# One more chunk's sums on TensorE and GpSimd, and preference for ten chunks' split steps, in a convolution with routed experts

## Chip, core and metric

The kernel runs on one core of a Trainium2 chip. The metric is the device time of one execution in microseconds (us). A profile of one execution goes with it: what every engine did and waited for.

## What is computed

Two stages. The first is a convolution over 7 past rows whose weights differ per token and head (a softmax over the 7 taps); the second sends each token to the one of 8 experts with the largest logit, and weights that expert's result with its softmax share.

```
B, S, D = 8, 3584, 192          # 28672 tokens; H = 8 heads of 24, K = 7 taps
w = softmax(weight_gen)                                        # (B, S, H, K)
x1[b, s, h] = sum_k w[b, s, h, k] * x_pad[b, s + k, h]         # 24 wide
logits = x1 @ w_gate                                           # 8 experts
e = argmax(logits);  gate = softmax(logits)[e]
out = gate * (relu(x1 @ w1[e]) @ w2[e])                        # 192 -> 1024 -> 192
```

## The kernel before, in words

**Tiling.** The tokens are cut into 28 chunks of 1024 (128 partitions with 8 tokens each), counted from 0 here: the fourth chunk is chunk 3. A chunk goes through three kinds of steps.

*Sums* (`taps`, `tap_ops`). The softmax weights `wp`, then for each of the 7 taps a product `x_sb * wp`. For a chunk from `HELP` on, VectorE (DVE) makes all 8 tokens' products (7 of 128x1536, lines 354) and adds them up itself (6 adds, line 378). For a chunk below `HELP`, VectorE makes only the products of 6 tokens (7 of 128x1152), TensorE (PE) adds them up by multiplying each with an identity into three PSUM tiles `ph` (line 363, 42 matmuls), and GpSimd (POOL) makes products and adds of the last two tokens (`wg`, `tp`, `acc`: 14 operations).

*Split* (`split`: `high`, then `low`). ScalarE (ACT) casts the sums to 16 bits into the row `pl` (line 448, or 444 from PSUM); VectorE writes what is left over (lines 461 and 463); TensorE transposes the 24 blocks (line 473), ScalarE copies them to `xg` (line 475).

*Finish* (`finish`). TensorE makes the logits in `pm` (line 485), VectorE routes (lines 492 to 507), counts and places, GpSimd sends the chunk's rows to the queues of the 8 experts in HBM (`send`, line 559, 8 indirect DMAs), and VectorE selects which tiles of tokens are now full (`choose`, the row numbers `rows`, line 599).

**Experts.** A tile has 256 tokens up to chunk 4 and 384 after it. SyncE (SP) loads its transposed rows `xt`, the expert's weights `wt` (1.8 MB, three buffers) and `meta`; TensorE makes the hidden layer (line 805) and the second layer (line 711), ScalarE takes results out of PSUM. A full tile needs 2040 waiting tokens while tiles have 256, more than 3064 with 384, so that chunk 1 gives one tile, chunks 2, 3 and 4 give four each, chunk 5 none and chunk 6 three.

**Weights.** All experts' weights are first split into two 16-bit parts by ScalarE (lines 271 and 272) and VectorE (lines 278 and 280), and written to `wq` in HBM (lines 285 to 290). This stretch, in which the first chunks are made too, is called the prologue here. A load of `wt` waits for all of `wq`.

**What sets the order.** A planner (`vector_step`) with a clock for VectorE and one for TensorE decides in which order the steps are written. In the prologue the framework then orders every engine by priorities and a simulated timeline; afterwards VectorE keeps the written order (`manual_schedule`) and the other engines are still ordered by the framework. `tc.high_priority()` puts the instructions written under it ahead of others that could go at the same time, on every engine that the framework orders. Only the finish steps ("route") are written under it. Each engine then works through its order and stops at an instruction whose input is not there.

The places that the change touches:

```
HELP = 3                                             # line 34
n = (J - POOL_COLS if c < HELP else J) * H           # line 342: tokens in wp
if c >= HELP:                                        # line 387: all on VectorE
```

Of the kernel before, what the change touches and what calls it, by code (L numbers as in the profile page):

```python
# [30 lines left out]
NCAP = 1 << 15  # L31
J = 8
POOL_COLS = 2
HELP = 3
EARLY = 5
STEP = 0.2
HURRY = 0.3
# [19 lines left out]
EXP_AT = 4  # L57
SC_AT = 7
MX_FROM = 3
SQ = 4  # L60
PROB = 3
TV = 2
# [51 lines left out]
def conv_moe_kernel(ctx: ExitStack, tc: tile.TileContext, x, wgen, w_gate, w1, w2, out):  # L114
# [203 lines left out]
    def soft0(c):  # L318
        k = ch[c]
        mx = cw.tile([P, J * H], F32, name="mx")  # L320
        nc.vector.tensor_reduce(mx, k.w, axis=AX.X, op=ALU.max)  # L321
        nc.gpsimd.tensor_tensor(k.w, k.w, mx.unsqueeze(2).to_broadcast([P, J * H, KW]), op=ALU.subtract)  # L322

    def soft1(c):
        nc.scalar.activation(ch[c].w, ch[c].w, AF.Exp)
# [12 lines left out]
    def soft3(c):  # L338

        k = ch[c]  # L340
        k.wp = ps_w.tile([P, J * H, KW], F32, name="wp")
        n = (J - POOL_COLS if c < HELP else J) * H
        nc.vector.tensor_tensor(k.wp[:, 0:n], k.w[:, 0:n], k.rs[:, 0:n].unsqueeze(2).to_broadcast([P, n, KW]),
                                op=ALU.mult)

    def tap_ops(eng, k, a, b, nm, aps):

        ac = k.acc[:, a:b, :].rearrange("p a (h g) -> p (a h) g", h=H)

        def mult(n, out):  # L350
            xs = k.x[:, a + n:b + n, :].rearrange("p a (h g) -> p (a h) g", h=H)
            w = k.wg if eng is nc.gpsimd else k.wp[:, a * H:b * H]
            ws = w[:, :, n:n + 1].to_broadcast([P, (b - a) * H, G])
            eng.tensor_tensor(out, xs, ws, op=ALU.mult)  # L354

        if aps is not None:
            for n in range(KW):
                t = cw.tile([P, (b - a) * H, G], F32, name=nm, bufs=TV)
                mult(n, t)
                tf = t.rearrange("p a g -> p (a g)")  # L360
                for i, ap in enumerate(aps):
                    m = min(2, b - a - 2 * i) * D
                    nc.tensor.matmul(ap[:, 0:m], identf, tf[:, 2 * i * D:2 * i * D + m],  # L363
                                     start=(n == 0), stop=(n == KW - 1))
                    clock[1] += 4 * m / 2400.0
                yield
            return
        mult(0, ac)
        yield
        t = cw.tile([P, (b - a) * H, G], F32, name=nm, bufs=TV)  # L370
        mult(1, t)
        yield
        for n in range(2, KW + 1):
            if n < KW:
                t2 = cw.tile([P, (b - a) * H, G], F32, name=nm, bufs=TV)
                mult(n, t2)
                yield
            eng.tensor_tensor(ac, ac, t, op=ALU.add)  # L378
            if n < KW:
                t = t2  # L380
            yield

    def taps(c):
# [4 lines left out]
        k.aps = None  # L388
        if c >= HELP:
            for _ in tap_ops(nc.vector, k, 0, J, "tv", None):  # L390
# [15 lines left out]
    def square(c, n, m):  # L406

        k = ch[c]

        def one(half, i, col, m):  # L410
            junk = cw.tile([P, m * D], BF16, name="junk", bufs=1, padded_shape=[P, J * D])
            v = k.x[:, col:col + m, :].rearrange("p a d -> p (a d)")
            nc.scalar.activation(junk, v, AF.Square, accum_out=ssqs[:, half, i:i + 1])  # L413

        if c == 0 and n == 0:
            one(1, 0, 0, HALO)
        one(c % 2, n // 2, HALO + n, m)
# [242 lines left out]
    def sums():  # L660
# [9 lines left out]
        for c in range(NCH):  # L670
# [4 lines left out]
            for cost in taps(c):  # L675
                n += 1
                if n <= 2 and c + 1 < NCH:
                    for i in range(4 * n - 4, 4 * n, SQ):
                        square(c + 1, i, SQ)
                yield cost, None  # L680
                if c + 1 < NCH:
                    if n == 2 and c + 1 < MX_FROM + 2:
                        soft0(c + 1)
                        yield 0.6, None
                    if n == EXP_AT:
                        soft1(c + 1)
                    if n == MX_AT and MX_FROM <= c < NCH - 2:

# [203 lines left out]

    def advance(queue_, what, after):
        at, g, c = queue_[0]
        with tc.high_priority() if what == "route" else nullcontext():
            lat = next(g, None)
        if lat is None:
            done[what] = c
            queue_.pop(0)
            if after:  # L900
                after(c)
        else:
            lat, cost = lat if isinstance(lat, tuple) else (lat, OP)
            clock[0] += cost
            queue_[0][0] = clock[0] + lat

    def vector_step():
# [12 lines left out]
        if routes and routes[0][0] <= now + (HURRY if routes[0][2] < SOON else 0.0):  # L920
            clock[0] = max(now, routes[0][0])
            advance(routes, "route", None)
            return True
        if splits and splits[0][0] <= now and splits[0][2] - done["route"] <= SPLITS:
            advance(splits, "split", lambda c: routes.append([clock[0], finish(c), c]))
            return True
# [77 lines left out]
```

## Time and profile before

| | us |
|---|---|
| median of 3 runs | 1240.84 |
| lowest to highest | 1239.42 to 1244.1 |
| profiled execution, its own time | 1242.18 |
| span of that execution in the trace | 1240.5 |
| PE busy | 1133.4 |
| DVE busy | 1036.7 |
| ACT busy | 696.8 |
| POOL busy | 660.6 |

The rows that the prediction uses come from that one execution. Times in them are counted from the start of the span; the 1.7 us between the span and the execution's own time lie outside it. A busy PE has a matmul under way, which is not the same as PE at its peak.

### The profile page before, as it was taken

To read this page: it belongs to the slowest core of one execution; us is meant where nothing else is said; L and a number is where in the kernel's file an instruction comes from. 1 tells how busy PE (TensorE), PEld (TensorE's weight loads), DVE (VectorE), ACT (ScalarE), POOL (GpSimd) and SP (SyncE) were. 2 spreads that over 40 slices of the span, in tenths; PEclk is the share of its full clock that TensorE was granted. 3 is DMA by queue.
4 is the path that set the end of the run, shared out by engine and by line. 5 is a ranking of instruction groups with operands and counts; after the bars stand their busy time and mean duration, and the time that the engine had idled before them with its cause. 6 is when DMAs were issued, how large, how long until landed. Compare 5 with 4: busy or idle time off the path is not lost.

```text
span 1240.5 us, 30087 instructions
## 1 busy us (share of the span) xinstructions
PE 1133.4 (91%) x11621; PEld 927.2 (75%) x11621; DVE 1036.7 (84%) x1849; ACT 696.8 (56%) x1459; POOL 660.6 (53%) x562
## 2 busy tenths in 40 slices
PE   5692189997999999999999999999999998999997
PEld 3461179896678788778788787787777786789997
DVE  7999966999999999999999999999998976232331
ACT  3455167675566666656756666656655663543442
POOL 6850853666656565446755565656464656222222
PEclk9896599999999999999999999999999999999998
DMA  9996698897768878787798878878776667999995
GB/s 277 346 323 241 232 282 264 287 304 236 232 201 267 265 230 250 238 234 235 247 277 237 237 227 255 247 240 254 239 215 178 191 197 222 340 348 348 321 362 218
DMA packets 185133, 320.93 MB, mean 259 GB/s; under 512 B 132752, under 2 KB 156434, under 8 KB 169118
## 3 DMA queue, kind: packets, MB, share of 16 engines
q1 hardware_dynamic: 162862, 273.68, 70.8%
q0 software_dynamic: 22128, 45.33, 11.1%
q8 instruction: 91, 1.49, 0.5%
q14 instruction: 52, 0.43, 0.1%
HBM read 236.17 MB, written 60.76 MB: 239 GB/s over the span
## 4 chain that ended last, share of the span: by engine, by line
PE 63%; DVE 13%; DMA 10%; issue 7%; POOL 4%; SPq 1%; ACT 1%; POOLq 0%; DVEq 0%; ACTq 0%
PE ph L805 29%; PE y L711 27%; DVE tv L354 4%; DVE acc L378 3%; DMA wt<-wq 3%; PE ph L473 2%; PE ph L818 2%; DMA f<-in_moe_w_dram 2%; POOL out_dram L559 2%; DMA xt<-queue 2%; DMA queue<-pl,pos 2%; DVE hl L828 1%; POOL queue L559 1%; PE ph L363 1%; PE pm L485 1%
## 5 line engine op out<-in xcount | busy, mean ns | idle before, releaser
L805 PE MATMUL ph<-xt,wt 128*128 128x384 f16 (+6 forms) x3880 | 578.8, 292 | 24.5 <-DMA wt<-wq 16.8
L711 PE MATMUL y<-wt,hh 128*128 128x192 f16 (+2 forms) x3696 | 504.5, 247 | 2.1 <-ACT o L715 2.1
L559 POOL DMA_INDIRECT out_dram<-o,meta x231 | 288.5, 1249 | 394.6 <-ACT o L715 349.0
L711 PE MATMUL y<-wt,hl 128*128 128x192 f16 (+2 forms) x1848 | 450.3, 247 | 0.4 <-ACT hl L820 0.2
L805 PEld LDWEIGHTS <-wt 128*128 128x128 f16 x3880 | 329.3, 98 | 144.4 <-DMA wt<-wq 18.9
L711 PEld LDWEIGHTS <-hh 128*128 128x128 f16 (+2 forms) x3696 | 337.0, 99 | 35.9 <-issue 5.0
L559 POOL DMA_INDIRECT queue<-pl,pos x224 | 286.8, 1280 | 118.1 <-issue 56.7
L828 DVE SCALAR_TENSOR_TENSOR hl<-ph,hh 128x384 f16<-128x384 f32 (+2 forms) x372 | 204.2, 562 | 144.2 <-ACT hh L825 139.0
L354 DVE TENSOR_TENSOR tv<-x_sb,wp 128x1536 f32<-128x1536 f32 (+1 forms) x171 | 289.0, 1693 | 3.9 <-PE ph L363 3.7
L825 ACT ACTIVATE hh<-ph 128x384 f16<-128x384 f32 (+2 forms) x372 | 185.5, 501 | 181.0 <-PE ph L805 170.4
L378 DVE TENSOR_TENSOR acc<-acc,tv 128x1536 f32<-128x1536 f32 x150 | 261.8, 1745 | 0.0
L711 PEld LDWEIGHTS <-hl 128*128 128x128 f16 (+2 forms) x1848 | 181.7, 98 | 16.5 <-ACT hl L820 1.4
L814 ACT ACTIVATE hh<-ph 128x384 f16<-128x384 f32 (+1 forms) x204 | 105.2, 518 | 84.7 <-PE ph L805 82.0
L715 ACT ACTIVATE o<-y,fac 128x192 f32<-128x192 f32 (+2 forms) x231 | 91.7, 418 | 89.4 <-PE y L711 83.4
L820 ACT ACTIVATE hl<-ph 128x384 f16<-128x384 f32 (+1 forms) x204 | 104.1, 519 | 37.0 <-PE ph L818 36.4
L475 ACT ACTIVATE xg<-ph 128x1024 f16<-128x1024 f16 x84 | 83.9, 1027 | 24.3 <-PE ph L473 24.2
L473 PE MATMUL ph<-idh,pl 128*128 128x128 f16 x672 | 56.1, 225 | 25.4 <-ACT pl L448 15.8
L818 PE MATMUL ph<-hh,negi 128*128 128x384 f16 (+1 forms) x256 | 68.1, 304 | 1.7 <-ACT hh L814 1.6
L473 PEld LDWEIGHTS <-pl 128*128 128x128 f16 x672 | 44.5, 101 | 29.4 <-ACT pl L448 16.1
L363 PE MATMUL ph<-tv,identf 128*128 128x384 f32 x126 | 51.6, 553 | 7.6 <-DVE tv L354 7.3
L413 ACT ACTIVATE junk<-x_sb 128x768 bf16<-128x768 f32 (+2 forms) x56 | 48.0, 857 | 13.6 <-DMA x_sb<-in_x_dram 6.5
L322 POOL TENSOR_TENSOR w_sb<-w_sb,mx 128x448 f32<-128x448 f32 x28 | 29.7, 1062 | 45.5 <-DVE mx L321 43.6
(121 smaller groups left out, 780.7 us busy)
## 6 DMA issues: line engine op xcount, KB each, us to landing
wt<-wq SPq DMA_DIRECT2D x97, 1796.0 KB
x_sb<-in_x_dram SPq DMA_DIRECT2D x27, 1344.0 KB
w_sb<-in_weight_gen_dram SPq DMA_DIRECT2D x28, 224.0 KB
wq<-ws SPq DMA_DIRECT2D x8, 772.0 KB
f<-in_moe_w_dram SPq DMA_DIRECT2D x8, 768.0 KB
f<-in_moe_w_dram SPq DMA_DIRECT2D x8, 512.0 KB
wq<-ws SPq DMA_DIRECT2D x8, 512.0 KB
wq<-ws SPq DMA_DIRECT2D x32, 128.0 KB
```

The lines of the kernel that those rows point to most:

```text
L354: eng.tensor_tensor(out, xs, ws, op=ALU.mult)
L378: eng.tensor_tensor(ac, ac, t, op=ALU.add)
L473: nc.tensor.transpose(pt[:, m, :], p16[:, j, n * P:(n + 1) * P], idh)
L559: st = nc.gpsimd.indirect_dma_start(out=dst, out_offset=bass.IndirectOffsetOnAxis(ap=idx, axis=0), in_=src, in_offset=None, **kw)
L711: nc.tensor.matmul(y, hx[:, f, sl], w2v[:, f, t, :], start=(f == 0 and k == 0), stop=(f == NF - 1 and k == 2))
L715: nc.scalar.activation(o[0:m, :], y, AF.Copy, scale=fac[0:m, s:s + 1])
L805: nc.tensor.matmul(ph[:, g], wt[:, wc + f * P:wc + (f + 1) * P], xt[:, xc, 0:T], start=(k == 0 and g == 0), stop=(k == 4), skip_group_chec ...
L814: nc.scalar.activation(hv, ph, AF.Relu, scale=SHRINK)
L818: nc.tensor.matmul(ph[:, g], negi, hv[:, g], start=False, stop=True, skip_group_check=True)
L820: nc.scalar.activation(lv, ph, AF.Relu)
L825: nc.scalar.activation(hv, ph, AF.Relu)
L828: nc.vector.scalar_tensor_tensor(lv, ph, 0.0, hv, op0=ALU.max, op1=ALU.subtract)
```

## The change

`HELP` goes from 3 to 4, so that chunk 3 too is summed by TensorE, with its last two tokens on GpSimd. A new constant `FRONT` of 10 puts the split steps of chunks 0 to 9 (and the steps of finishing, as before) under the priority. What is written under `advance` with `what` "split" are `high` and `low`.

```diff
-HELP = 3
+HELP = 4
...
+FRONT = 10
...
     def advance(queue_, what, after):
         at, g, c = queue_[0]
-        with tc.high_priority() if what == "route" else nullcontext():
+        with tc.high_priority() if what == "route" or c < FRONT else nullcontext():
             lat = next(g, None)
```

From line 60 on a line of the changed kernel has a number that is one higher.

The first place is ScalarE's order around the casts of chunk 4 (`pl_132`), the first chunk that is split after the experts have begun. Before, with line 814 for a first half of a hidden layer, 820 for its second, 715 for a result:

```order
L814 ACTIVATE hh<-ph 128x2x256 x3
L715 ACTIVATE o<-y,fac 128x192
L820 ACTIVATE hl<-ph 128x2x256
L814 ACTIVATE hh<-ph 128x2x256
L820 ACTIVATE hl<-ph 128x2x256 x2
L325 ACTIVATE w_sb<-w_sb 128x448
L715 ACTIVATE o<-y,fac 128x192
L820 ACTIVATE hl<-ph 128x2x256
L842 ACTIVATE fac<-meta,wt 128x2
L814 ACTIVATE hh<-ph 128x2x256
L448 ACTIVATE pl_132<-acc 128x4x192 x2
```

The casts stood behind nine `hh` and two results, in the third tile. ScalarE's order at the same place in the changed kernel:

```order
L843 ACTIVATE fac<-meta,wt 128x2
L815 ACTIVATE hh<-ph 128x2x256 x3
L821 ACTIVATE hl<-ph 128x2x256
L326 ACTIVATE w_sb<-w_sb 128x448
L815 ACTIVATE hh<-ph 128x2x256
L821 ACTIVATE hl<-ph 128x2x256 x3
L815 ACTIVATE hh<-ph 128x2x256 x2
L449 ACTIVATE pl_132<-acc 128x4x192 x2
```

They now stand behind six `hh` and no result, in the middle of the second tile.

The second place is VectorE's order at the end of the prologue, around the last split of weights (`ws_178`, the eighth expert; `pos`, `lm`, `lg`, `pri`, `se`, `oh`, `eq` are routing). Before:

```order
L378 TENSOR_TENSOR acc<-acc,tv 128x1536
L544 TENSOR_REDUCE pos<-rk 128x8
L579 MAX top<-cand 1x8
L270 TENSOR_TENSOR ws_178<-nin 128x1
L495 TENSOR_REDUCE lm<-lg 128x8
L278 SCALAR_TENSOR_TENSOR ws_178<-f_942,nsc,ws_178 128x1536
L378 TENSOR_TENSOR acc<-acc,tv 128x1536
L343 TENSOR_TENSOR wp<-w_sb,sm 128x448
L584 TENSOR_TENSOR eq<-cand,top 1x64
L497 TENSOR_TENSOR lg<-lg,lm 128x64
L280 SCALAR_TENSOR_TENSOR ws_178<-f_943,nsc,ws_178 128x8x192
```

Chunk 3's last adds stood between the last weights. Now:

```order
L355 TENSOR_TENSOR tv<-x_sb,wp 128x1536 x2
L498 TENSOR_TENSOR lg<-lg,lm 128x64
L212 TENSOR_SCALAR nsc<-nbits 128x2
L213 TENSOR_SCALAR nin<-nbits 128x2
L379 TENSOR_TENSOR acc<-acc,tv 128x1536
L502 SCALAR_TENSOR_TENSOR pri<-lg,revE 128x64
L271 TENSOR_TENSOR ws_178<-nin 128x1
L522 TENSOR_REDUCE se<-eg 128x8
L355 TENSOR_TENSOR tv<-x_sb,wp 128x1536
L279 SCALAR_TENSOR_TENSOR ws_178<-f_942,nsc,ws_178 128x1536
L505 TENSOR_REDUCE pmx<-pri 128x8
L281 SCALAR_TENSOR_TENSOR ws_178<-f_943,nsc,ws_178 128x8x192
```

The products (`tv`) and the add (`acc`) in these rows are chunk 4's: all of chunk 3's work on VectorE is done, and chunk 4 is five operations in, when the last weights are split.

## Rows read from the trace of the kernel before

**Rows 1.** Stretches: length, busy us (instructions) of PE, PEld, DVE, ACT, POOL; PE clock; DMA.

```profile
100.00:120.00 20.00, 2.92 (x51) 2.39 (x48) 20.00 (x30) 6.80 (x9) 0.97 (x1) 0.59 0.49 176
120.00:140.00 20.00, 3.52 (x33) 2.89 (x33) 20.00 (x38) 7.71 (x8) 14.36 (x6) 0.50 0.74 255
```

**Rows 2.** TensorE's waits from 96 to 156 us: total, times, longest.

```profile
PE pm L512 <- DVE oh L507: 14.5, 3, 7.7
```

**Rows 3.** TensorE's waits from 155 to 346 us.

```profile
PE ph L805 <- DMA wt<-wq: 15.3, 5, 10.0
PE ph L473 <- ACT pl L448: 3.5, 1, 3.5
PE ph L805 <- DMA xt<-queue: 2.7, 2, 2.3
PE ph L473 <- DVE pl L461: 2.1, 1, 2.1
```

**Rows 4.** TensorE's waits from 346 us to the end.

```profile
PE ph L805 <- DMA xt<-queue: 3.4, 1, 3.4
```

**Rows 5.** VectorE's waits from 130 to 346 us.

```profile
DVE pl L461 <- ACT pl L448: 12.5, 2, 10.8
DVE lg L492 <- PE pm L485: 12.2, 3, 9.8
```

**Rows 6.** VectorE's waits from 346 to 1045 us.

```profile
DVE hl L828 <- ACT hh L825: 11.9, 14, 2.1
DVE lg L492 <- PE pm L485: 9.5, 6, 6.1
```

**Rows 7.** VectorE by line and shape, 90 to 127 us: busy, mean ns | idle before.

```profile
L354 DVE TENSOR_TENSOR tv<-x_sb,wp 128x1536 f32<-128x1536 f32 x6 | 10.5, 1747 | 0.0
L378 DVE TENSOR_TENSOR acc<-acc,tv 128x1536 f32<-128x1536 f32 x6 | 10.4, 1738 | 0.0
```

**Rows 8.** VectorE by line and shape, 14 to 88 us.

```profile
L354 DVE TENSOR_TENSOR tv<-x_sb,wp 128x1152 f32<-128x1152 f32 x20 | 26.8, 1346 | 3.8 <-PE ph L363 3.7
```

**Rows 9.** GpSimd by line and shape, 53 to 70 us, the columns of chunk 2.

```profile
L378 POOL TENSOR_TENSOR acc<-acc,tp 128x384 f32<-128x384 f32 x6 | 6.0, 1008 | 0.1
L354 POOL TENSOR_TENSOR tp<-x_sb,wg 128x384 f32<-128x384 f32 x6 | 5.3, 894 | 0.2
```

**Rows 10.** TensorE by line and shape, 74 to 96 us: the sums of chunk 2.

```profile
L363 PE MATMUL ph<-tv,identf 128*128 128x384 f32 x42 | 15.3, 498 | 2.0 <-DVE tv L354 1.8 <-issue 0.2
```

**Rows 11.** The page: the sends to the queues, by GpSimd.

```profile
L559 POOL DMA_INDIRECT queue<-pl,pos x224 | 286.8, 1280 | 118.1 <-issue 56.7
```

**Rows 12.** SyncE in order of time from 129 us: start, length, DMA issued.

```profile
129.97 0.38 SPq L286 DMA_DIRECT2D wq<-ws  x1
144.14 1.33 SPq L743 DMA_TRANSPOSE xt<-queue  x1
145.95 0.39 SPq L745 DMA_DIRECT2D wt<-wq  x1
```

**Rows 13.** Stretches of 2 us, columns as in the earlier table.

```profile
132.00:134.00 2.00, 1.70 (x15) 1.50 (x16) 2.00 (x6) 0.40 (x1) 2.00 (x1) 0.50 1.03 423
138.00:140.00 2.00, 0.48 (x9) 0.39 (x8) 2.00 (x5) 0.00 (x0) 1.95 (x1) 0.50 0.00 0
```

**Rows 14.** TensorE in order of time, from 155 and from 311 us [wait before].

```profile
155.27 1.03 PE L805 MATMUL ph<-xt,wt 128*128 128x256 f16 x4 [9.99 <-DMA wt<-wq]
...
311.60 1.81 PE L805 MATMUL ph<-xt,wt 128*128 128x384 f16 x5
...
315.26 0.97 PE L805 MATMUL ph<-xt,wt 128*128 128x384 f16 x5
```

**Rows 15.** VectorE's leftover operation, a window at 35 and one at 74 us: ns.

```profile
L461 DVE TENSOR_TENSOR pl<-acc,pl x1: 1079/1079/1079, 34.9 to 34.9; 128x256 f16<-128x256 f32 x1
...
L461 DVE TENSOR_TENSOR pl<-acc,pl x1: 411/411/411, 74.2 to 74.2; 128x256 f16<-128x256 f32 x1
```

**Rows 16.** VectorE in order of time: the first split beside experts [wait before].

```profile
177.52 0.69 DVE L461 TENSOR_TENSOR pl<-acc,pl 128x512 f16<-128x512 f32 x1 [10.76 <-ACT pl L448]
```

## The prediction

> **What bounds the kernel now.** I read the table of stretches first, then the lists of waits, then the instructions in order of time around the places that the lists name. The span falls into three parts. From 100 us until the experts start TensorE has almost nothing to do: 2.9 and 3.5 us of work in the two stretches of 20 us, at a granted clock near 0.5 (the 1.2 GHz level), while VectorE is busy for 20.0 of 20 in both [rows 1]. What TensorE waits for there is mostly VectorE: 14.5 us for the routing masks `oh` alone [rows 2]. So VectorE paces the first 150 us. From 155 to 346 us TensorE runs experts and waits in short pieces: 5.3 us for weights (15.3 less the 10.0 that end with the experts' start), 5.6 in front of the transposes of chunk 8 (3.5 for ScalarE's casts, 2.1 for VectorE's leftovers), and 2.3 for the first tile of chunk 6 [rows 3]. After 346 us it waits for little; the longest is 3.4 us for the last chunk's rows [rows 4]. From there to the end the time is TensorE's own work. VectorE is no second bound: it loses 22 us between 130 and 346 us, waiting for ScalarE's casts of chunk 4 (10.8) and for its logits (9.8) [rows 5], and it has over 20 us of waits between 346 and 1045 us [rows 6]. A change therefore pays if it starts the experts earlier or removes a TensorE wait before 346 us, and what it adds to TensorE costs nothing before the start and its full length after it.
>
> **Chunk 3 on TensorE and GpSimd.** Removed from VectorE: 7 products of 1747 ns and 6 adds of 1738 ns [rows 7], 22.6 us. Added: 7 products of 1346 ns [rows 8], 9.4 us. VectorE gains 13.2 us, and about 1 us more because only two of the chunk's eight tokens leave it a leftover to make. GpSimd gets 14 operations: 6 adds and 6 products took 6.0 and 5.3 us for chunk 2 [rows 9], with the first product and the weights about 14 us. By the order they stand ahead of chunk 0's sends, which then go some 10 us later; nobody reads a chunk's rows before chunk 1 gives its first tile, so that costs nothing. TensorE gets 42 matmuls, 15.3 us of work [rows 10], and three more. They lie before the experts' start, where TensorE has 30 of 40 us free; if that cover were gone they would cost all 15.3.
>
> How much earlier do the experts start? The first tile needs chunk 1's rows in the queue and all of `wq`. Counting VectorE's instructions of both orders up to the last split of weights, the changed kernel has there 7 products of 1152 more (9.4 us), 3 products of 1536 fewer (5.2) and 5 adds fewer (8.7), and about 2 us of small routing steps more: 2.5 us less in all, because five operations of chunk 4 have moved ahead of it. So the last weights leave VectorE only 2 or 3 us earlier at best. What moves more is chunk 1: its places come about 15 us earlier in the sum of VectorE's work, and its eight sends of 1.28 us [rows 11] can follow. Before, SyncE issued the last part of `wq` at 129.97 us, stood until 144.14 us for the sends to land and only then loaded the first rows and, at 145.95, the first weights [rows 12]. The DMA engines, at a share of 1.03 at 132 us, had nothing to do at 138 us [rows 13]: `wq` had landed by 136 us, and some 10 us passed with both VectorE's weights and the DMA engines done. With chunk 1's sends landed by about 130 us, `wq` is last in the changed kernel, at 134 to 137 us. The load took 9.3 us from its issue to the first matmul at 155.27 [rows 12, 14], so the experts start at 143.5 to 147; I take 145, **10 us earlier**. Bounds: 12 us, with `wq` at 134; and 3 us, if GpSimd delays VectorE or the sends stay last.
>
> The upper end of that delay is in the rows: beside GpSimd's columns one leftover operation of VectorE took 1079 ns, and without them 411 [rows 15]. Four weight splits and two leftover operations lie beside chunk 3's columns; at 0.7 us each that is 4 us. I take 1, since most of them come after the columns are through. The Trainium skill speaks against the change here (SBUF — State Buffer, Who interferes with whom): a VectorE instruction with two SBUF inputs and a GpSimd instruction that reads SBUF shut each other out for a whole instruction. The trace agrees, 1079 ns against 411. By that rule alone the start would come at 149 and not 145, and the sum would be 4 us smaller.
>
> **Preference for the split steps.** It adds no instruction. Counting the columns of expert matmuls that stand ahead of a chunk's transposes in TensorE's order, chunk 4's move from 58,900 to 22,900, chunk 5's from 115,700 to 80,100, chunk 8's from 265,200 to 256,400; from chunk 9 on the two orders differ by little. Before, VectorE reached chunk 4's leftovers and stood 10.76 us, until 177.52 [rows 16], because ScalarE's casts were queued behind nine expert results; now they stand behind six. With the start at 145, these come at about 155, when VectorE, whose work up to there is 13 us shorter, arrives too (about 154). So both long waits of VectorE [rows 5] mostly go, and from chunk 4 on it runs about 20 us earlier and in step with TensorE. What is queued behind the preferred instructions is the experts' own work on TensorE and ScalarE: a few us per chunk, done earlier instead of later, not more of it.
>
> What that gives TensorE: chunk 6's tiles came 2.3 us too late for it [rows 3]. VectorE is 25 to 30 us earlier there and TensorE 10, so this wait goes: **2.3 us**. In front of chunk 8's transposes 5.6 us go the same way. Behind that wait the clock was at its lower level: five matmuls of 384 columns took 1.81 us at 311.60 and 0.97 at 315.26 [rows 14], some 6 us of work at half speed; so 3 us more go with the wait: **8.6 us**. Bounds for these two together: 0, if the waits only move to another chunk, and 13, if the short waits for weights and results shrink too. The waits for weights after the start (5.3 us, the 15.3 of [rows 3] less the 10.0) stay: there are three buffers, and a load takes 9 us. So does the 3.4 us at the end [rows 4].
>
> **The sum.** 1242.2 (the profiled execution) - 10 - 2.3 - 8.6 = 1221. The median of the runs is 1.3 us under that execution, so I predict **1220 us**, 1.7% less.
>
> **Rivals.**
> - *The start is held back.* GpSimd's columns push VectorE's last weights back by 4 us, or ScalarE splits the eighth expert late, because chunk 3's preferred casts stand ahead of it in its order; the start gains 3 to 5 us and the rest stays: 1226. For it: the margin between ScalarE and VectorE there is under 2 us in my sum. Against it: most of the columns lie where GpSimd had nothing to do and VectorE made products that were no slower. The rule of the Trainium skill named above (SBUF — State Buffer, Who interferes with whom) is one way into this rival.
> - *The preferred steps stall TensorE (slower).* Each engine stops at the next instruction in its order. Chunk 8's transposes cost 5.6 us of waiting and 3 at the lower clock; should all six preferred chunks beside experts (4 to 9) cost these 8.6, it is 52 us on top of the forecast: 1272. Should only two, 1237. It decides when VectorE reaches chunk 4's leftovers later than TensorE its transposes, 12 us after the start; my sum has 154 against 157. Against it: a stall delays TensorE once, and VectorE, at 28 to 30 us for a chunk, then is ahead. It ends above 1247 only with four or more such stalls, 1254 with four.
> - *The gain is given back.* The start moves 3 us, and the waits at chunks 6 and 8 come back at other chunks, or the tail's wait of 3.4 us grows by what was gained, as the last chunk's rows then come late: about 1238, the same. Against it: VectorE's own 20 us of waits after 346 us [rows 6].
> - *More than that.* The tail's wait and the waits for weights go too: 1210.
>
> **How the numbers follow.** A difference under 0.5% (6 us) cannot be told from no change here. The forecast, 1212 to 1225, gets 0.57; the held-back start, 1225 to 1230, 0.17; more than that 0.07; given back 0.10; the stalls that end slower 0.09. Faster: 0.57 + 0.17 + 0.07 = 0.81. Same 0.10, slower 0.09. The range from 1209 to 1231 holds the first two and most of the third, about 0.8.
>
> **What would show it.** In the profile of the changed kernel: the first `ph` matmul on `xt` near 145 us; the 42 more sums before it; VectorE's wait for chunk 4's casts under 4 us and for its logits under 3; no wait of TensorE in front of `L474` transposes between 250 and 330 us, and a clock of 1.00 there; after 346 us the same stretches as before, some 20 us earlier. The forecast is wrong if the first expert matmul comes after 152 us, if transposes appear in TensorE's list of waits with more than 5 us, or if TensorE's waits after 346 us exceed 15 us.

## The result and the profile after

The changed kernel takes **1224.4 us** (median of 4 runs, 1221.2 to 1226.5) against 1241.7 us before: ratio 0.987, 95% interval 0.985 to 0.989. It is faster by 17 us; 1220 was predicted, with a range of 1209 to 1231. The profiled execution took 1224.1 us, its span 1222.4, against 1242.2 and 1240.5 before.

Eight of the twelve runs below were made on chips where every kernel took 8 to 10% longer (the kernel before 1363 and 1346 us), because the engines stood there again and again for about 1 us with nothing to wait for; so every ratio is against the kernel before on the same chip, and the ledgers come from the other chips.

First TensorE's and VectorE's lists of waits of the changed kernel, as in [rows 3, 5]: who waited for whom, us in total, how often, the longest. The longest come first and shorter ones are left out.

```profile
PE ph L806 <- DMA wt<-wq: 16.1, 6, 11.9
PE ph L819 <- ACT hh L815: 4.6, 1, 4.6
PE ph L806 <- ACT o L716: 0.5, 1, 0.5
```

```profile
DVE pl L462 <- ACT pl L449: 11.9, 3, 10.4
DVE tv L355 <- PE ph L364: 7.7, 5, 2.6
DVE lg L493 <- PE pm L486: 3.6, 2, 3.1
```

TensorE's list is that of 140 to 340 us, VectorE's of 20 to 340. The transposes (3.5 and 2.1 us) and the late rows of chunk 6 (2.3) are gone from TensorE's list [rows 3]; a wait of 4.6 us for a result of ScalarE is new. VectorE still waits 10.4 us for chunk 4's casts.

The next rows are stretches of 20 us of the changed kernel and, the second pair, of the kernel before: length, busy time of PE, PEld, DVE, ACT, POOL with instructions, granted clock, DMA share, GB/s.

```profile
160.00:180.00 20.00, 17.22 (x174) 14.77 (x174) 10.14 (x11) 12.98 (x23) 3.44 (x4) 0.83 0.64 210
...
300.00:320.00 20.00, 20.00 (x193) 15.39 (x191) 17.44 (x33) 12.34 (x31) 9.26 (x9) 1.00 0.69 220
```

```profile
160.00:180.00 20.00, 18.00 (x179) 15.95 (x177) 9.17 (x12) 14.34 (x29) 9.28 (x9) 1.00 0.96 224
...
300.00:320.00 20.00, 14.35 (x128) 9.86 (x126) 20.00 (x34) 11.37 (x22) 14.29 (x10) 0.74 0.91 291
```

From 300 to 320 us TensorE now works without a gap at a granted clock of 1.00 (the 2.4 GHz level), where before it had 14.35 us at 0.74. From 160 to 180 us it is the other way: 0.83, where before it was 1.00.

**Where the 18.1 us of span came from.** ScalarE scales each tile's factors once (`fac`), so these rows count tiles. The 13th and the 24th tile, of before (line 842) and of after (843):

```profile
289.94 0.30 ACT L842 ACTIVATE fac<-meta,wt 128x2 f32<-128x2 f32 x1
...
452.81 0.30 ACT L842 ACTIVATE fac<-meta,wt 128x3 f32<-128x3 f32 x1
```

```profile
290.61 0.29 ACT L843 ACTIVATE fac<-meta,wt 128x2 f32<-128x2 f32 x1
...
438.43 0.30 ACT L843 ACTIVATE fac<-meta,wt 128x3 f32<-128x3 f32 x1
```

At tile 13 the changed kernel is 0.7 us *behind*, at tile 24 it is 14.4 ahead. In both kernels TensorE has made the same transposes by tile 13 (96 since 140 us). The time between the marks divides into time in which TensorE was busy and time in which it was not. First matmul on expert rows to tile 13, then tile 13 to 24, before and after (columns as in the last table):

```profile
155.27:289.94 134.67, 128.51 (x1433) 118.14 (x1434) 109.92 (x163) 92.87 (x182) 75.26 (x58) 0.99 0.88 280
289.94:452.81 162.87, 152.00 (x1462) 118.42 (x1460) 162.05 (x290) 98.31 (x215) 92.23 (x73) 0.97 0.78 238
```

```profile
149.86:290.61 140.75, 131.59 (x1436) 120.04 (x1436) 127.98 (x195) 95.18 (x188) 79.75 (x61) 0.96 0.86 276
290.61:438.43 147.82, 147.48 (x1456) 117.20 (x1457) 142.22 (x253) 93.41 (x207) 83.20 (x69) 1.00 0.83 255
```

- *To tile 13:* the start is 5.4 us earlier (below), and the stretch behind it is 6.1 us longer: 3.0 us more idle and 3.1 us more busy. Idle: 4.6 for the new wait and 0.5 for results, less 1.4 for weights (5.3 to 3.9) and 0.4 for rows. Busy, with almost the same number of matmuls: behind the new wait TensorE worked 5.6 us, from 162.6 to 168.2, at the lower level of its clock (0.50 granted), which by this count costs about 2.8 us. So the new wait costs about 7.4 us in all.
- *Tile 13 to 24:* 15.1 us shorter. Idle time falls from 10.9 to 0.3 us: 2.3 for rows, 5.6 in front of the transposes and 2.7 for results are gone. Busy time falls by 4.5 us; about 3.3 of it is work that the kernel before did at the lower level (6.7 us of work between 305.0 and 315.2), in and behind the waits in front of its transposes.
- *After tile 24:* 3.7 us, of which 2.0 are idle time. Two waits of the kernel before are gone, for `hh` (1.6) and `hl` (0.8); the last chunk's rows cost 0.5 less and weights 1.0 more. No row assigns the rest.

So the gain lies around chunk 8, and the earlier start was spent within 13 tiles.

**The start, 5.4 us earlier and not 10.** The columns of these rows are start, length, engine, line, operation, tiles, and in brackets the idle time before and who ended it. First the last split of weights before, then that of the changed kernel with its first matmul on expert rows.

```profile
127.75 1.80 DVE L280 SCALAR_TENSOR_TENSOR ws<-f,nsc,ws 128x1536 f16<-128x1536 f32 x1
```

```profile
131.32 1.80 DVE L281 SCALAR_TENSOR_TENSOR ws<-f,nsc,ws 128x1536 f16<-128x1536 f32 x1
...
149.86 5.95 PE L806 MATMUL ph<-xt,wt 128*128 128x256 f16 x32 [11.90 <-DMA wt<-wq]
```

VectorE's last weight split ends at 133.1 us, 3.6 later than before (129.5) and not 2 or 3 earlier. VectorE's busy time up to that end, before and after (third number behind the length):

```profile
0.00:129.55 129.55, 74.00 (x508) 48.64 (x508) 119.12 (x199) 61.17 (x93) 69.53 (x86) 0.86 0.91 299
```

```profile
0.00:133.12 133.12, 90.27 (x576) 57.84 (x577) 117.41 (x210) 65.35 (x104) 86.47 (x106) 0.91 0.89 296
```

It worked 1.7 us less (2.5 were counted) and stood 5.3 us longer: 15.7 us against 10.4.

SyncE issued the last part of `wq` until 134.96 and the first rows at 138.84, and the first matmul followed 11 us later. Chunk 1's sends did not hold it, as forecast: the last was issued at 124.34. Between the two SyncE reads the row numbers (`rows`) of three tiles of chunk 2, which stand ahead of chunk 1's first rows in its order. VectorE had written them at 136.40. SyncE's list of waits names an instruction near it; the second row is that of chunk 3's sums alone (e1r_help4 below):

```profile
SPq L732 <- DVE pri L502: 2.0, 1, 2.0
```

```profile
SPq L731 <- DVE lg L497: 5.3, 1, 5.3
```

So the weights were not the last thing that the start waited for. No kernel with another order of these reads was tried.

The reason why VectorE came late stands 60 us ahead, in four engines' rows in order of cause:

```profile
65.51 2.42 DVE L279 SCALAR_TENSOR_TENSOR ws<-f,nsc,ws 128x1536 f16<-128x1536 f32 x1
...
66.27 2.53 POOL L379 TENSOR_TENSOR acc<-acc,tp 128x384 f32<-128x384 f32 x1
...
69.52 1.83 DVE L281 SCALAR_TENSOR_TENSOR ws<-f,nsc,ws 128x1536 f16<-128x1536 f32 x1
...
69.70 2.51 POOL L379 TENSOR_TENSOR acc<-acc,tp 128x384 f32<-128x384 f32 x1
...
73.53 0.52 ACT L449 ACTIVATE pl<-acc 128x384 f16<-128x384 f32 x1 [4.72 <-POOL acc L379]
...
74.54 2.93 PE L364 MATMUL ph<-tv,identf 128*128 128x384 f32 x4 [3.81 <-ACT pl L454]
...
77.50 1.35 DVE L355 TENSOR_TENSOR tv<-x_sb,wp 128x1152 f32<-128x1152 f32 x1 [2.04 <-PE ph L364]
...
80.98 1.35 DVE L355 TENSOR_TENSOR tv<-x_sb,wp 128x1152 f32<-128x1152 f32 x1 [1.74 <-PE ph L364]
```

GpSimd makes chunk 2's two columns. Two of its adds take 2.5 us instead of 1.0, each beside a weight split of VectorE; the first of these splits takes 2.42 us instead of 1.80, the second 1.83. ScalarE's cast of these columns stands ahead of chunk 1's last casts in its order and waits 4.72 us. Those casts hold the PSUM tiles that TensorE's sums of chunk 3 need: 3.81 us. VectorE's products of chunk 3 need the buffers that the sums hold: 2.04 and 1.74 us. Before, VectorE summed chunk 3 itself, and none of this could reach it.

**The new wait** is read the same way:

```profile
159.50 0.96 POOL L560 DMA_INDIRECT queue<-pl,pos  x1 [0.30 <-issue]
160.49 0.97 POOL L323 TENSOR_TENSOR w_sb<-w_sb,mx 128x448 f32<-128x448 f32 x1
...
161.50 0.58 ACT L326 ACTIVATE w_sb<-w_sb 128x448 f32<-128x448 f32 x1 [4.79 <-POOL w_sb L323]
161.98 0.58 ACT L815 ACTIVATE hh<-ph 128x512 f16<-128x512 f32 x1
...
162.61 0.58 PE L819 MATMUL ph<-hh,negi 128*128 128x256 f16 x2 [4.61 <-ACT hh L815]
```

The softmax of chunk 6 needs a subtraction on GpSimd, whose input VectorE had ready at 151.4 us. It stood behind the 16 sends of chunks 2 and 3, the last of them at 159.50. ScalarE's exp waited for it with the first tile's fourth result `hh` queued behind, and TensorE for that.

One effect of the change I had not seen in the diff: chunk 5's subtraction and its maximum are gone (27 of each instead of 28). They are written at the 11th step of chunk 3's sums, and a chunk summed on TensorE has only 8 steps. A softmax does not change by it; it saves one operation of 0.6 us on VectorE and one of 1.0 on GpSimd. What it is worth alone was not tried.

### The profile page after: what moved, and what is told of

It is laid out like the page before. It is cut to its first block, busy times and chain, and to the rows that moved or that the text cites. A ratio compares the mean times of both kernels' runs of the same rounds, so it can differ in the third digit from the quotient of the medians.

```text
span 1222.4 us, 30194 instructions
## 1 busy us (share of the span) xinstructions
PE 1143.8 (94%) x11666; PEld 933.4 (76%) x11666; DVE 1025.9 (84%) x1840; ACT 697.5 (57%) x1467; POOL 660.1 (54%) x575
## 4 chain that ended last, share of the span: by engine, by line
PE 66%; issue 14%; DMA 8%; POOL 5%; DVE 4%; ACT 1%; SPq 1%; POOLq 0%; DVEq 0%; ACTq 0%
PE ph L806 30%; PE y L712 27%; POOL out_dram L560 4%; DMA wt<-wq 4%; PE ph L474 3%; PE ph L819 2%; PE ph L364 2%; DMA f<-in_moe_w_dram 1%; DVE tv L355 1%; POOL queue L560 1%; PE pm L486 1%; DVE ws L281 1%; DMA queue<-padrow,padi 1%; DMA x_sb<-in_x_dram 1%; DMA queue<-pl,pos 1%
## 5 line engine op out<-in xcount | busy, mean ns | idle before, releaser
L560 POOL DMA_INDIRECT out_dram<-o,meta x231 | 285.7, 1237 | 379.4 <-ACT o L716 339.4
L560 POOL DMA_INDIRECT queue<-pl,pos x224 | 276.5, 1234 | 120.2 <-issue 63.8
L379 DVE TENSOR_TENSOR acc<-acc,tv 128x1536 f32<-128x1536 f32 x144 | 250.0, 1736 | 0.0
L712 PEld LDWEIGHTS <-hl 128*128 128x128 f16 (+2 forms) x1848 | 181.5, 98 | 15.7 <-ACT hl L821 0.4
L364 PE MATMUL ph<-tv,identf 128*128 128x384 f32 x168 | 68.1, 544 | 14.6 <-DVE tv L355 10.7
L364 PEld LDWEIGHTS ph<-tv,identf 128*128 128x128 f32 x168 | 32.8, 210 | 34.9 <-DVE tv L355 13.3
L414 ACT ACTIVATE junk<-x_sb 128x768 bf16<-128x768 f32 (+2 forms) x56 | 48.0, 857 | 14.4 <-DVE ssq L423 6.8
L474 PE MATMUL ph<-idh,pl 128*128 128x128 f16 x672 | 53.4, 220 | 1.2 <-ACT xg L476 0.5
L449 ACT ACTIVATE pl<-acc 128x768 f16<-128x768 f32 (+1 forms) x52 | 40.0, 811 | 21.0 <-DVE acc L379 16.3
```

What stands on the lines that cost most here:

```text
L560: st = nc.gpsimd.indirect_dma_start(out=dst, out_offset=bass.IndirectOffsetOnAxis(ap=idx, axis=0), in_=src, in_offset=None, **kw)
L712: nc.tensor.matmul(y, hx[:, f, sl], w2v[:, f, t, :], start=(f == 0 and k == 0), stop=(f == NF - 1 and k == 2))
```

## Experiments

All twelve runs, with the ratio to the kernel before on the same chip and its interval:

| run | median us (before) | ratio |
|---|---|---|
| e1_help4: chunk 3's sums alone | 1348.8 (1363.0) | 0.986 (0.978 to 0.995) |
| e1r_help4: the same | 1220.8 (1240.1) | 0.984 (0.981 to 0.987) |
| e2_front10: preference alone | 1368.2 (1363.0) | 1.004 (1.000 to 1.008) |
| e2r_front10: the same | 1356.9 (1346.0) | 1.008 (1.005 to 1.011) |
| after_again: both halves | 1330.0 (1346.0) | 0.989 (0.984 to 0.994) |
| e3_from4: both, preference from chunk 4 | 1320.3 (1346.0) | 0.982 (0.978 to 0.986) |
| e6_cut2: both, columns of chunk 2 cut | 1347.0 (1363.0) | 0.987 (0.980 to 0.993) |
| e10_behind: both, columns' cast behind | 1221.0 (1240.1) | 0.983 (0.980 to 0.986) |
| e7_sub6: both, one subtraction moved | 1349.0 (1363.0) | 0.987 (0.979 to 0.994) |
| e7r_sub6: the same | 1220.5 (1240.1) | 0.985 (0.981 to 0.989) |
| e12_help4_sub6: chunk 3's sums, subtraction moved | 1319.1 (1346.0) | 0.977 (0.971 to 0.983) |
| e12r_help4_sub6: the same | 1217.2 (1242.5) | 0.978 (0.975 to 0.981) |

### Which half carries the gain

Each half alone, against the kernel before:

```
-HELP = 3                                             # e1_help4, e1r_help4
+HELP = 4
...
-        with tc.high_priority() if what == "route" else nullcontext():     # e2_front10, e2r_front10
+        with tc.high_priority() if what == "route" or c < FRONT else nullcontext():
```

> Only the first half of the change: chunk 3's sums on TensorE and GpSimd, no preference for split steps. Theory (the two halves carry different parts): the earlier start comes from here, so the first expert matmul lies at 148 to 152 us (155.3 before, 149.9 with both halves), while the transposes of chunk 8 still wait for casts or leftovers (5.6 us before): about 1232 to 1236. Rival (VectorE's 13 us alone remove the waits in front of transposes, the preference is idle): no such wait above 1 us, and 1222 to 1226, as with both.

> Only the second half: preference for the split steps of chunks 0 to 9, with chunk 3's sums on VectorE. Theory: the start stays within 2 us of 155, the waits in front of chunk 6's tiles and chunk 8's transposes (2.3 and 5.6 us and 3 us of half clock) go: 1230 to 1234. Rival (without VectorE's 13 us the preferred transposes come before VectorE has made their leftovers, and TensorE stands in front of them): transposes in TensorE's list of waits with more than 5 us in all, 1238 to 1248.

The first runs gave 0.986 and 1.004, with wide intervals; both were run again.

> Chunk 3's sums on TensorE and GpSimd alone, without the preference, a second time on a chip where, I hope, nothing else stops the engines. The first run gave ratio 0.986 with an interval of 0.978 to 0.995, the same as both halves. Theory by that run (this half carries nearly all of it, the preference nothing): 0.985 to 0.989. Rival (the recorded one, in which the waits in front of chunks 6 and 8 go with the preference): 0.991 to 0.996, with over 4 us of TensorE's waits between the start and 346 us for chunk 8's casts or leftovers.

> Only the preference for the split steps of chunks 0 to 9, chunk 3's sums on VectorE, a second time. Theory (the preference carries nothing by itself: chunk 3's sums alone gave 0.984): ratio 0.996 to 1.004, start at 154 to 158 us. Rival (the recorded one: it removes the waits in front of chunk 6's tiles and chunk 8's transposes): 0.990 to 0.994, with no transposes among TensorE's waits of over 1 us.

Chunk 3's sums alone give 0.984, at least as much as both halves. TensorE's waits of e1r_help4 from 140 to 340 us:

```profile
PE ph L805 <- DMA wt<-wq: 16.6, 6, 11.3
PE ph L805 <- ACT hl L820: 4.4, 1, 4.4
```

No transposes, no late rows: both waits went without the preference, as the rival in e1_help4's expectation had it. Its 4.4 us are the same subtraction behind the same sends. VectorE begins chunk 8's leftovers at 285.7 us, against 289.6 with both halves and 308.0 before. The first expert matmul lies at 145.87 us, 4.0 earlier than with both halves, and tile 24 at 432.70 us, 5.7 earlier. These are two single executions on two chips; the ratios, 0.984 and 0.987, have intervals that overlap.

The preference alone makes the kernel slower, 1.008 with an interval above 1. There the transposes still wait. From TensorE's list of e2r_front10, 140 to 350 us:

```profile
PE ph L474 <- ACT pl L449: 2.4, 1, 2.4
...
PE ph L474 <- DVE pl L462: 1.6, 1, 1.6
```

These are 4.0 us, under the 5 that e2_front10's rival wanted, and the same list has 4.4 us for late rows; the recorded theory of that run (1230 to 1234) is wrong, its rival right in the sign. The start came at 162.84 us, outside the 154 to 158 of e2r_front10's expectation (157.41 in e2_front10). Where the rest of the 11 us went was not followed: the kernel before has no trace on that chip.

### The preference of the early chunks

```
-        with tc.high_priority() if what == "route" or c < FRONT else nullcontext():
+        with tc.high_priority() if what == "route" or HELP <= c < FRONT else nullcontext():
```

> The changed kernel as it is, on the same chip as the three that follow, so that they can be set beside it. Both theories: 1222 to 1226, ratio to the kernel before 0.985 to 0.989; first expert matmul at 147 to 150, one wait of TensorE of about 4.6 us for a result of ScalarE near 158 us.

> The changed kernel with the preference for chunks 4 to 9 alone, not for 0 to 3. Theory (the preference of the early chunks costs the start 2 to 4 us, and that of the later ones gives nothing measurable): start at 145 to 147 us, ratio 0.981 to 0.986, as with chunk 3's sums alone (0.984). Rival 1 (the later chunks' preference is worth the recorded 11 us of waits in part): 0.975 to 0.980. Rival 2 (the early preference is harmless): start at 148 or later, 0.985 to 0.989.

On this chip the changed kernel started its experts at 155.80 us and e3_from4 at 148.50; the ratios are 0.989 and 0.982, and the intervals just overlap. But these two starts can't be set against each other: in after_again ScalarE's casts near 100 us stood 6.3 us in all, in the one execution that was profiled, with nothing in the profile of this core that ended the waits. The longest of the three:

```profile
103.51 0.38 ACT L453 ACTIVATE pl<-ph 128x256 f16<-128x256 f32 x1 [4.57 <-remote]
```

What the early preference costs the start is better read on the chips without such stops: 149.86 us and 147.76 with it (the changed kernel and e7r_sub6 below, whose orders are the same up to there), 145.87 and 146.14 without (e1r_help4 and e12r_help4_sub6). That is 2 to 4 us, from four single executions. In e1r_help4 VectorE waits 2.1 us for TensorE's sums from 20 to 134 us, and not 7.7: without the preference ScalarE's cast of the columns waits 1.7 us there and not 4.72, and the chain above hardly forms.

The first numbers of after_again's expectation, 1222 to 1226 and a start of 147 to 150, failed, on a chip where every kernel is slower; its ratio fits. e3_from4's ratio is that of its theory, its start 1.5 us later than the theory's. With the preference of chunks 4 to 9 left, 0.982 is what chunk 3's sums alone gave (0.984, 0.986): from there it gives nothing that these runs can tell from nothing.

### GpSimd's columns and the start

First, 8 of GpSimd's 14 operations for chunk 2 left out, from the changed kernel, so that two of its eight tokens get only part of their sums:

```
-        rest = tap_ops(nc.gpsimd, k, pc, J, "tp", None)
+        rest = islice(tap_ops(nc.gpsimd, k, pc, J, "tp", None), 5 if c == 2 else 99)
```

> The changed kernel without 8 of GpSimd's 14 operations for chunk 2's last two tokens (their sums take two of seven taps, so these tokens' results are left wrong). Theory: the start came at 149.9 and not at 145 because GpSimd ends chunk 2's columns only at 73 us, ScalarE's cast of them waits 4.7 us with the casts of chunk 1's remainders behind it, TensorE's sums of chunk 3 wait 3.8 us for these and VectorE's products 3.8 us for the sums. Then here: no wait of ScalarE for acc above 1 us near 70, VectorE's waits for sums before 134 us at 4 us or less (7.7 before), last weight split done at 127 to 130 us (133.1), first expert matmul at 144 to 147, 1218 to 1221. Rival (the eleven more instructions in VectorE's order and slower small ones beside GpSimd delay the split, the waits do not matter): split at 132 or later, start 148.5 or later, 1223 to 1226.

ScalarE's wait for the columns fell from 4.72 to 0.79 us, and VectorE's waits for sums from 7.7 to 2.8; but the start came at 152.4, and the split at 134.7. A row of ScalarE shows why this says nothing on the start:

```profile
100.11 0.38 ACT L453 ACTIVATE pl<-ph 128x256 f16<-128x256 f32 x1 [5.30 <-remote]
```

A gap of 5.3 us that nothing in the profile ended lies in the same chain of casts, as in after_again. Inconclusive. On another chip, with all the work done and only this order asked for (the framework then moved other instructions too):

```
-                nc.scalar.activation(hi, ap, AF.Copy)
+                behind = nc.scalar.activation(hi, ap, AF.Copy)
...
+            if k.aps:
+                tc.add_manual_dep(cast.ins, behind.ins.name, wait_for, ...)
```

> The changed kernel, where ScalarE's cast of a chunk's two GpSimd columns must stand behind the casts of that chunk's sums in its order, so that chunk 2's columns no longer hold up chunk 1's casts; every operation is done. Theory (GpSimd's late columns delay the start by way of ScalarE and TensorE's sums): TensorE's 3.8 us wait for casts near 74 us gone, VectorE's waits for sums before 134 us under 4.5 us (7.7), first expert matmul at 145 to 147.5 (149.9), ratio 0.982 to 0.985. Rival (VectorE's own work sets the start): start at 149 or later, ratio 0.986 to 0.989.

Its last split and first expert matmul, VectorE's busy time up to the end of that split, and TensorE's waits from 140 to 340 us:

```profile
122.41 1.80 DVE L281 SCALAR_TENSOR_TENSOR ws<-f,nsc,ws 128x1536 f16<-128x1536 f32 x1
...
142.17 5.65 PE L808 MATMUL ph<-xt,wt 128*128 128x256 f16 x32 [8.10 <-DMA wt<-wq]
```

```profile
0.00:124.21 124.21, 92.21 (x596) 58.80 (x596) 112.83 (x215) 64.41 (x103) 91.07 (x108) 0.94 0.96 318
```

```profile
PE ph L808 <- DMA wt<-wq: 18.9, 7, 8.1
PE ph L821 <- ACT hh L817: 1.8, 1, 1.8
```

TensorE's 3.81 us wait is gone, the split comes 8.9 us earlier, the start 7.7 (142.17), more than expected. Only part of this is the chain. VectorE stood 11.4 us up to the end of the split and not 15.7: 4.3 us. Its waits for sums are 4.6 us (7.7), just above the 4.5 expected. The other 4.6 us are work that no longer stands ahead of the split: four of chunk 4's five operations of 128x1536 moved behind it, less some small ones that moved ahead. So the order asked for takes the wait away, but how much of the 8.9 us it is worth by itself this run doesn't show. And the time is hardly lower (0.983 with 0.980 to 0.986, against 0.987 with 0.985 to 0.989): after the start TensorE waits 10.8 us for weights (18.9 less 8.1), where the changed kernel waits 4.2.

A cleaner case is the next kernel, unasked: its orders up to the experts' start are those of the changed kernel, yet in e7r_sub6 only one of the two adds met a split. Its rows:

```profile
65.90 1.00 POOL L379 TENSOR_TENSOR acc<-acc,tp 128x384 f32<-128x384 f32 x1
...
68.05 2.52 POOL L379 TENSOR_TENSOR acc<-acc,tp 128x384 f32<-128x384 f32 x1
```

ScalarE's cast then waited 1.63 us and not 4.72, TensorE's sums 0.4 and not 3.8, and the last split came at 128.36 and not 131.32. With the same order of every engine, one such meeting less goes with a shorter chain and a split 3 us earlier; its start is 2.1 us earlier (147.76). It is one execution of each.

### The one subtraction

Moved to VectorE, first in the changed kernel:

```
-        nc.gpsimd.tensor_tensor(k.w, k.w, mx.unsqueeze(2)...
+        (nc.vector if c == 6 else nc.gpsimd).tensor_tensor(k.w, k.w, mx.unsqueeze(2)...
```

> The changed kernel with the subtraction of the maximum for chunk 6 on VectorE, right behind the maximum, instead of GpSimd. Theory: TensorE's 4.6 us wait for ScalarE's result at 158 us comes from this one subtraction, which stands behind 16 sends on GpSimd; here the wait goes, and with it 2 to 3 us at half clock; VectorE pays 0.6 to 1.0 us: 1216 to 1220, TensorE's granted clock in 160 to 180 us above 0.95 (0.83). Rival (the wait only moves: VectorE comes later to chunk 4's leftovers, or TensorE then waits for the same 5 us for weights or rows of the next tiles): 1222 to 1226.

> The changed kernel with the subtraction of the maximum for chunk 6 on VectorE instead of GpSimd, a second time: in the first run all engines stood for some us again and again with nothing to wait for, in every kernel, and the kernel before took 1363 us there. Theory (one subtraction behind 16 sends costs TensorE 4.6 us of waiting and 2 to 3 at half clock): ratio to the kernel before 0.979 to 0.984, 6 to 8 us less than the changed kernel's 0.987. Rival (the wait only moves): 0.985 to 0.989.

The first run told nothing (0.979 to 0.994). In the second the wait for ScalarE is gone:

```profile
PE ph L806 <- DMA wt<-wq: 22.5, 6, 12.8
```

This is all that TensorE waits for from 140 to 340 us. But 9.7 of it lie after the start (4.2 in the changed kernel): the wait moved to the weights, as the rival had it. The ratio, 0.985 with 0.981 to 0.989, lies between theory and rival and can't decide. The granted clock of 160 to 180 us is 0.95 (0.83).

Then in the kernel without the preference:

> Chunk 3's sums on TensorE and GpSimd, no preference, and chunk 6's subtraction on VectorE. There, without it, TensorE waited 4.4 us for ScalarE near 155 us. Theory: that wait goes, but a part comes back as waits for weights, which arrive every 9 to 11 us while a tile of 256 rows takes TensorE about as long: TensorE's waits for weights after the start 5 to 10 us (5.3), ratio 0.979 to 0.983. Rival (all of it comes back): 0.983 to 0.986, waits for weights 10 us or more. Second rival (none comes back): 0.978 or less.

> Chunk 3's sums on TensorE and GpSimd, no preference, chunk 6's subtraction on VectorE, a second time; the first run (ratio 0.977) was on a chip where the engines stop again and again with nothing to wait for. Set beside chunk 3's sums alone on a quiet chip (0.984; start 145.9 us, then one wait of 4.4 us for ScalarE and 5.3 us for weights). Theory (the one subtraction costs 4.4 us, and half of that or more comes back as waits for weights): start within 2 us of 146, no wait of over 2 us for ScalarE before 340 us, waits for weights after the start 6 to 11 us, 1215 to 1219, ratio 0.979 to 0.983. Rival (nothing comes back): weights 5.5 us or less, 1214 or less. Second rival (all comes back): 1219 or more, ratio 0.984 or more.

The first expert matmul of e12r_help4_sub6 and TensorE's waits from 140 to 340 us:

```profile
146.14 5.72 PE L805 MATMUL ph<-xt,wt 128*128 128x256 f16 x32 [11.33 <-DMA wt<-wq]
```

```profile
PE ph L805 <- DMA wt<-wq: 17.7, 7, 11.3
PE y L711 <- ACT hl L820: 1.0, 1, 1.0
```

The start is e1r_help4's, the 4.4 us for ScalarE are 1.0, and the weights take 6.4 after the start (5.3): little came back. The ratios, 0.977 and 0.978, lie just under the theory's 0.979 to 0.983, where the second rival of the first run had them (none comes back); the median of the second run, within the theory's 1215 to 1219, is 3.6 us under e1r_help4's, on another chip. This kernel is faster than the kernel before and the changed one: 1217 us, its interval of 0.975 to 0.981 below the changed kernel's 0.985 to 0.989.

## Why the prediction was right, and where it was not

The time is right in part by luck. Of the 21 us in the sum 18.1 came, but by other terms: the start gave 4.6 less and a wait that was not in the sum cost about 7.4, while gains that were not in the sum came to about 9 (3.7 of them after tile 24, the rest in shorter waits for results, weights and rows). The terms for rows and transposes came as sized, but not by the half of the change that they were ascribed to.

- **What bounds the kernel: right.** VectorE paced the first 150 us, the end is TensorE's own work, and the gain came from the two places named: the start and the waits before 346 us.
- **The start, 10 us: half.** 5.4 came, between the bounds of 3 and 12. The step that failed is the count of VectorE's instructions up to the last split, "2 or 3 us earlier": it was 3.6 later. Counting instructions took no new waits in. Those were 4.0 us more for TensorE's sums (7.7 against 3.7), and 1.8 for two casts and an exp of ScalarE. I had charged GpSimd's columns to VectorE's own instructions only, 1 us of 0 to 4, and these took 0.8 us more than counted. The larger effect was on GpSimd: its adds grew from 1.0 to 2.5 us, and a chain of three engines carried that to VectorE. The reads of chunk 2's row numbers ahead of the first rows were not in the sum either. By the rule that I named (the Trainium skill, SBUF — State Buffer, Who interferes with whom) a VectorE instruction with two inputs in SBUF and a GpSimd instruction that reads SBUF block each other. The trace agrees for the splits: both slow adds end 0.9 us after VectorE's split has ended, about the length of an add alone (1.00). It does not agree for the products, which have two inputs in SBUF too; neither engine is slower here:

```profile
61.31 1.34 DVE L355 TENSOR_TENSOR tv<-x_sb,wp 128x1152 f32<-128x1152 f32 x1
```

```profile
61.28 1.00 POOL L379 TENSOR_TENSOR acc<-acc,tp 128x384 f32<-128x384 f32 x1
```

- **The rival of the held-back start** (1226) came near: 1224.4, with a start gain just above its 3 to 5 us. The first of its two reasons holds in effect: the last weights came 3.6 us later than before (it had 4) because of GpSimd's columns, though by waits and not by slower instructions of VectorE. The second, preferred casts ahead of the eighth expert on ScalarE, was not it: the expert's first half was cast by 127.5 us, before VectorE took it up at 129.4. Casts that stand ahead of others do matter, but those of chunk 2's columns, 50 us earlier.
- **The preference: wrong.** It was to bring the transposes of chunks 4 to 8 in time, and with that 2.3 and 8.6 us. The waits went, with a clock of 1.00 there, as forecast, and their size was right: 2.3 for rows, 5.6 for transposes and about 3.3 for the clock. But they go without the preference too, and stay with the preference alone. What removes them is chunk 3's sums, with which VectorE comes to chunk 8 about 20 us earlier. Of the preference the runs show only a cost: 0.8% alone (1.008; the first run's 1.004 reaches down to none); beside chunk 3's sums, a later start and 5.7 us at tile 24, which the ratios do not tell from noise. The part of the argument that failed is the comparison of expert columns ahead of the transposes. It says how early TensorE asks for chunk 4's rows, not who comes last; VectorE's wait for those casts was 10.4 us, as long as before (10.8), where under 4 was forecast, and it ended at 169.8 us and not near 155. Its wait for logits was 3.6 us (under 3 forecast).
- **Terms not in the sum.** The wait of 4.6 us behind GpSimd's sends and its 2.8 us at the lower clock. I had asked of chunk 0's sends who reads their rows, and found nobody. Who stands behind the sends of chunks 2 and 3 in GpSimd's order I had not looked up: it is the subtraction for chunk 6.
- **The waits for weights "stay": not in general.** They were 4.2 us here (5.3 forecast), but 9.7 and 10.8 in the two kernels of both halves that started earlier or lost the wait for ScalarE. There an earlier start was worth less than its us.
- **After 346 us** the same tiles came 14.4 us earlier (tile 24), not some 20.
- **A reading:** VectorE's two waits of [rows 5] come to 24.7 us, not 22; nothing hangs on it.

## What to carry to other kernels

Price a step that is moved to another engine by what stands behind it in that engine's order, DMA issues included, and not only by what reads its result. Try the parts of a change alone: here one half gave as much as the whole and the other made the kernel slower when tried alone, while the sum looked as forecast. When the work after a start is fed by loads that take as long as a tile, measure a gain some tiles later, not at the start.

## What the runs showed of the hardware

- GpSimd and VectorE can delay each other both ways: a GpSimd add of 128x384 took 1.00 us alone and 2.51 to 2.53 beside a weight split, and one of the two splits 2.42 instead of 1.80. Beside VectorE's products of 128x1152 (1.34 us) the same add took 1.00. One such meeting more or less went with 3 us of difference in the last split between two kernels with the same order up to there.
- Chips differ. On two of the four that the experiments ran on, engines stopped through the whole run with nothing to wait for; of TensorE's waits in after_again from 360 to 1000 us, where the same kernel had none at all on the chip of its first runs:

```profile
PE y L712 <- issue: 7.6, 17, 1.0
```

What makes them stop stays open.
